# Moving weight preparation, a decay chain of one operation less, and two sets of folded DFT inputs in a fused attention, gated and mixing kernel

## The chip, the cores and the metric

The kernel runs on one core of a Trainium2 chip. The metric is the device time of one execution, in microseconds. Lower is better. The engines are TensorE (PE, with its weight loads shown as PEld), VectorE (DVE), ScalarE (ACT), GpSimd (POOL) and SyncE (SP), which here issues nearly all DMAs.

## The reference

Three layers run one after the other on 4 batches of 576 tokens. The first is causal attention with 8 heads of 64 dimensions, where a score also gets a decay: the difference of running sums of log f.

```python
cum = np.cumsum(np.log(np.clip(f, 0.0001, 1.0)), axis=-1)
scores = scale * np.matmul(q, k.transpose(0, 1, 3, 2)) + cum[:, :, :, None] - cum[:, :, None, :]
attn_out = softmax(where(causal, -1e9, scores)) @ v
# gated layer, d_ff = 1024, conv = 3 taps over the tokens
h = np.maximum(x @ w_in, 0.0)
y = (h * sigmoid(conv(h, conv_w))) @ w_out
# mixing layer
u = y + np.real(fft(fft(y, axis=1), axis=2))
out = u + np.maximum(layernorm(u) @ w_ch1, 0.0) @ w_ch2
```

The weights are double precision in memory, and the kernel turns them into single precision on the chip ("decode").

## The kernel before

**Stages.** Attention runs over 16 pairs of heads: `score` (L688) does the score matmuls and the exponentials, `trans` (L750) transposes the probabilities and `pv` (L788) multiplies them by v. The decay enters the scores as a second matmul against `cum`, a tile made once at the start (L607 to L613): clip, logarithm, running sum, a product with -8, a rounded copy on ACT, and for two strips of 32 rows the remainder that the rounding left. After each four pairs (one batch) `bc_chunks` (L815) adds 24 chunks to a queue, which the loop feeds in between the pairs: 8 chunks `b_chunk` (x @ w_in, convolution, gate) and 16 halves of chunks `c_chunk` (the product with w_out). The result goes to memory as `z_d`. Then `dft` (L955) makes u for each batch: it loads `zz` tiles, folds them into `zo` and splits each into a rounded and a remainder part in `zh` (L963 to L972), multiplies `zh` by the DFT's matrices, evacuates to `ab`, multiplies again (`pq`), and writes u to `u_d`. The last part is the channel layer over chunks of 512 tokens (`prep_u`, `ch1`, `ch2`), with the fourth batch's DFT worked in.

**Weights.** `load_w_in` (L626) and `load_w_out` (L632) each handle one of 8 units. A unit is one DMA of 512 KB, then `decode` (one ACT and four DVE operations on 128x512), then for w_in a rounded copy on ACT and a remainder on POOL. For w_out there are, besides, a sum and a difference of mirrored columns (POOL and DVE) and a DMA that stores the unit to `wo_d`, from which `c_chunk` loads it again. `prep` (L894 to L897) hands two units of w_in to each of the first four half-steps of the pair loop, and two of w_out to each of half-steps 6 to 9. The preparation of the first 7 of 16 slices of w_ch1 and w_ch2 follows from half-step 10.

**What orders the work.** Nothing is issued in the order of the code. Every operation is recorded, and a planner (`Plan.order`, L448) lists them: for each engine it takes, of the operations that are ready by its own table of costs, the one whose latest start is earliest. An operation with a `hold` is not ready before that planned time (nanoseconds), and one with a `lead` counts as more urgent. The outcome is a fixed order for each engine's queue, and each queue runs strictly in that order. So a change at any place can move work elsewhere.

**Memory.** The tiles of `dft` lie in the pool `dp`, which takes the place of the attention's tiles when those are free. `zh` is one tile, and four `zz` tiles rotate. The pool `mr`, which holds the channel layer's weights and its inputs `ux`, `uc`, `uh` and `ul`, takes the place of the gated layer's pools `bc` and `ga`.

Of the kernel before, what the change touches and what calls it, by code (L numbers as in the profile page):

```python
# [7 lines left out]
F32 = mybir.dt.float32  # L8
F32R = mybir.dt.float32r
I32 = mybir.dt.int32  # L10
U32 = mybir.dt.uint32
AF = mybir.ActivationFunctionType
ALU = mybir.AluOpType
# [9 lines left out]
CUTS = (0, 8, 16)  # L23
NMR, G3 = 7, (2, 2)
ULE, W2E = 'V', 'V'
NCV, NZZ, NZO, NX = 2, 4, 2, 5
NUO, NWARM = 1, 10
LASTW = 256
EV = (2, 4)
NTV = 4  # L30
NPT = 1
DRAIN = 200.0
NS, NU, NSPLIT = 4, 2, 4
NPB = 2
BK3 = (3,)
# [8 lines left out]
UW, ZW = DM + 2, 640  # L44
# [172 lines left out]
def cost_of(eng, fn, kw, subs=None):  # L217
    if subs:
        return DRAIN + sum(cost_of(eng, f, k) for f, k in subs) / 2
    o = kw["out"]  # L220
# [295 lines left out]
def build(tc, qk, v, f, w_in, conv, w_out, w_ch1, w_ch2, c_mask, c_ident, c_sgn, c_dd, c_ds, out):  # L516
    plan = Plan(tc)
    V, A, G, T, SP = (Engine(plan, n) for n in ("DVE", "ACT", "POOL", "PE", "SP"))

    def dma(out, in_):  # L520
        SP.dma_start(out=out, in_=in_)

    def hi(out_, in_):
        A.activation(out=out_, in_=in_, func=AF.Copy)

    def lo(eng, out_, in_, hi_):
        eng.tensor_tensor(out=out_, in0=in_, in1=hi_.bitcast(F32), op=ALU.subtract)
# [39 lines left out]
    dp = plan.pool("dft", after=[att])  # L567
# [9 lines left out]
    z_d = [dram.tile([4, 128, ZW], F32) for _ in range(B)]  # L577
# [9 lines left out]
    cum = att.tile([128, S], F32R)  # L587
# [12 lines left out]
    ft = att.tile([128, S], F32, tag="rb")  # L600
# [6 lines left out]
    V.tensor_scalar(out=ft, in0=ft, scalar1=1e-4, scalar2=1.0, op0=ALU.max, op1=ALU.min)  # L607
    A.activation(out=ft, in_=ft, func=AF.Ln)
    V.tensor_tensor_scan(out=ft, data0=one, data1=ft, initial=0.0, op0=ALU.mult, op1=ALU.add)
    V.tensor_scalar(out=ft, in0=ft, scalar1=-8.0, scalar2=None, op0=ALU.mult)  # L610
    A.activation(out=cum, in_=ft, func=AF.Copy)
    for i in (32, 96):
        lo(V, cum[i:i + 32], ft[i:i + 32], cum[i:i + 32])  # L613
    plan.lead = 0.0
    dma(out=mask, in_=c_mask)
    dma(out=ident, in_=c_ident)
# [5 lines left out]
    def load_conv():  # L622
        t = decode(wp, fetch(wp, conv, 3 * NFO), 3 * NFO)
        V.tensor_scalar(out=cw, in0=t, scalar1=2.0, scalar2=None, op0=ALU.mult)
# [37 lines left out]
    for par in range(2 * NPB):  # L662
        row = []
        for i in range(5):
            w = KW[i] + 64
            t = att.tile([128, w], F32)
# [222 lines left out]
    def bc_step():  # L889
        if queue:  # L890
            queue.pop(0)()

    load_conv()
    prep = {}  # L894
    for u in range(8):
        prep.setdefault(u // 2, []).append((load_w_in, u))
        prep.setdefault(6 + u // 2, []).append((load_w_out, u))  # L897
    clear_pads()
    for s in range(NP + 1):
        if 2 * s == SCST:  # L900
            plan.hold = 1e4 * SCST
            for i in range(2):
                G.dma_start(out=dd_d[:, i], in_=c_dd[:, i])
            for i in range(2):
                G.dma_start(out=ds_d[:, i], in_=c_ds[:, i])
            plan.hold = 0.0
        for x in (2 * s, 2 * s + 1):
            for fn, u in prep.get(x, []):
                fn(u)
            if 10 <= x < 10 + NST:  # L910
                plan.bias = 1e6
                for k in range(2):
                    dma(out=wch_d[2 * (x - 10) + k], in_=fetch_ch(k, x - 10))
                plan.bias = 0.0
        load(s + 1)
        if s < NP:
            load_v(s)
        for grps, tiles in (((4, 1), TX), ((3, 2), TY)):
            for grp in grps if s >= 1 else ():
                for n in (2 * s - 2, 2 * s - 1):  # L920
                    trans(n, grp)
                bc_step()
                bc_step()
            if s < NP:
                for part in (tiles[:1], tiles[1:]) if s < NSPLIT else (tiles,):
                    score(s, part)
        if s < NP:
            norm(s)
        if s >= 1:
            pv(s - 1)  # L930
            if s % (H // 2) == 0:
                queue.extend(bc_chunks(s // (H // 2) - 1))
# [7 lines left out]
    def load_consts():  # L940
        for i in range(2):
            dma(out=cdh[:, i], in_=dd_d[:, i])
        for i in range(2):
            dma(out=cst[:, i], in_=ds_d[:, i])
# [2 lines left out]
    TT = [(0, 128), (128, 128), (256, 64)]  # L947
    SK = (128, 128, 33)

    zh = dp.tile([128, 2, 4, 289], F32R)  # L950
    uos = [dp.tile([128, 257], F32) for _ in range(NUO)]
    for t in uos:
        V.memset(out=t[:, 0:257:256], value=0.0)

    def dft(b, bank):  # L955
        zz = []
        for c in range(4):
            t = dp.tile([128, ZW], F32, tag="zz", bufs=NZZ)
            dma(out=t, in_=Flat(z_d[b], 128 * ZW * c, [ZW, 128], [1, ZW]))
            zz.append(t)  # L960
        if b == 0:
            load_consts()
        for c in (2, 0, 1, 3):  # L963
            zo = dp.tile([128, 5, 64], F32, tag="zo", bufs=NZO)
            zF, zB = zz[c].over(0, [128, 5], [1, 64]), zz[c].over(64, [128, 5], [1, 64])
            if c == 2:
                V.scalar_tensor_tensor(out=zo, in0=zB, scalar=sgn, in1=zF, op0=ALU.mult, op1=ALU.add)
            else:
                G.tensor_tensor(out=zo, in0=zF, in1=zB, op=ALU.subtract if c == 3 else ALU.add)
            z1 = zo.over(0, [1, 289])  # L970
            hi(zh[:, 0, c], z1)
            lo(G, zh[:, 1, c], z1, zh[:, 0, c])  # L972
# [284 lines left out]
```

## Time and profile before

| | us |
|---|---|
| median of 3 runs | 906.49 |
| lowest and highest of them | 905.81, 908.7 |
| the profiled execution | 901.2 |
| its span, first to last instruction | 899.4 |
| PE busy in the span | 848.3 (94%) |
| DVE, ACT, POOL busy | 534.6, 375.4, 195.6 |

All rows come from the profiled execution. Times in them are microseconds from the start of the span. A busy PE says only that a matmul was under way, and "PEclk" is the share of TensorE's full clock that was granted. "DMA" is the mean busy share of the 16 DMA engines. A row of the busy times by stage gives the stretch, its length, then for each engine the busy time and the count of its instructions, then PEclk, the DMA share and GB/s. A row of a timeline gives the start, the duration, the engine, the line, the operation and the tiles it writes <- reads; the brackets at its end tell how long the engine had been idle before it and what ended that. A row of a group ends with the count, the busy time, the mean of one in nanoseconds, and the idle time before it.

### The profile page before, as it was taken

What the parts mean: (1) busy time and instruction counts of PE and PEld (TensorE: products, weight loads), DVE (VectorE), ACT (ScalarE), POOL (GpSimd) and SP (SyncE); (2) the same over time, 40 slices, a digit from 0 to 9 for tenths busy, and PEclk for the clock granted to TensorE, in tenths of its full rate; (3) what the DMA queues carried; (4) which work ended last, traced back from release to release, by engine and by line L of the source; (5) the groups of instructions that cost most, each with busy time, mean ns of one, the idle gap of its engine ahead of it and who ended that gap; (6) DMA issues with size and microseconds to landing.
All of it is one profiled execution on the core that took longest, in us unless ns stands there. A gap on an engine that the chain in (4) does not pass through costs nothing.

```text
span 899.4 us, 14182 instructions
## 1 busy us (share of the span) xinstructions
PE 848.3 (94%) x5148; PEld 710.7 (79%) x5148; DVE 534.6 (59%) x1413; ACT 375.4 (42%) x1002; POOL 195.6 (22%) x204
## 2 busy tenths in 40 slices
PE   7787989899999999999996899999999999999998
PEld 6455878779887888899985788888888888888897
DVE  6887998478963684368647788884535112411141
ACT  5775876368645675365434443332121111111111
POOL 1233252102310231059636621110000000000000
PEclk9698999999999999999998999999999999999999
DMA  6465446973376204496679465442313000200010
GB/s 214 146 191 177 174 147 219 384 236 125 122 224 205 92 17 126 141 285 176 201 205 226 136 173 184 151 154 58 107 24 95 1 0 1 94 1 0 32 63 24
DMA packets 75270, 119.87 MB, mean 133 GB/s; under 512 B 10392, under 2 KB 44984, under 8 KB 75200
## 3 DMA queue, kind: packets, MB, share of 16 engines
q1 hardware_dynamic: 74624, 116.01, 42.6%
q0 software_dynamic: 576, 2.95, 0.9%
q8 instruction: 40, 0.66, 0.3%
q14 instruction: 30, 0.25, 0.1%
HBM read 93.66 MB, written 27.70 MB: 135 GB/s over the span
## 4 chain that ended last, share of the span: by engine, by line
PE 49%; DMA 5%; DVE 4%; POOL 3%; issue 2%; ACT 1%; SPq 0%; DVEq 0%; POOLq 0%; ACTq 0%
PE psc_c__4978 L506 11%; PE psc_c__4977 L506 10%; PE psc_c__5070 L506 4%; PE psc_c__5069 L506 4%; PE psdft_x__4025 L506 4%; PE psdft_x__4024 L506 4%; PE psc_c__5072 L506 3%; PE psc_c__5071 L506 3%; PE psbc_bc__529 L506 2%; PE psbc_bc__528 L506 2%; DMA dram_t__380<-glu_t__145 1%; DMA dram_t__381<-dft_u__3909 1%; PE psatt_u__179 L498 1%; DMA wprep_dw__121<-dram_t__384 1%; POOL dft_u__3909 L506 1%
## 5 line engine op out<-in xcount | busy, mean ns | idle before, releaser
L506 DVE SCALAR_TENSOR_TENSOR mr_gl__4869<-psc_c__4977,mr_gh__4868 128x512 fp32r<-128x512 f32 (+1 forms) x40 | 25.4, 635 | 89.8 <-ACT mr_gh__4868 L506 89.7
L506 ACT ACTIVATE mr_gh__4868<-psc_c__4977 128x512 fp32r<-128x512 f32 (+1 forms) x40 | 22.2, 555 | 124.2 <-PE psc_c__4977 L506 121.7
L506 DVE SCALAR_TENSOR_TENSOR mr_gl__4873<-psc_c__4978,mr_gh__4872 128x512 fp32r<-128x512 f32 (+1 forms) x40 | 25.3, 633 | 81.2 <-ACT mr_gh__4872 L506 81.1
L506 ACT ACTIVATE mr_gh__4872<-psc_c__4978 128x512 fp32r<-128x512 f32 (+1 forms) x40 | 22.2, 554 | 119.6 <-PE psc_c__4978 L506 114.7
L506 DVE SCALAR_TENSOR_TENSOR glu_cv__162<-glu_t__143,bc_t__127,glu_cv__162 128x576 f32<-128x576 f32 x32 | 33.8, 1055 | 7.3 <-ACT glu_cv__162 L506 7.0
L506 DVE SCALAR_TENSOR_TENSOR glu_cv__163<-glu_t__144,bc_t__127,glu_cv__163 128x576 f32<-128x576 f32 x32 | 33.0, 1031 | 3.2 <-ACT glu_cv__163 L506 3.0
L506 DVE TENSOR_SCALAR wprep_dw__118<-wprep_dw__118 128x512 f32<-128x512 f32 (+1 forms) x25 | 13.3, 532 | 26.9 <-ACT wprep_dw__118 L506 26.8
L498 PE MATMUL psatt_s__175<-att_t__67,att_t__66 64*128 64x288 f32 (+2 forms) x48 | 27.1, 564 | 1.1 <-DVE att_t__67 L506 1.1
L498 PE MATMUL psatt_s__176<-att_t__67,att_t__66 64*128 64x288 f32 (+2 forms) x48 | 27.1, 565 | 0.3 <-DVE att_t__67 L506 0.3
L506 ACT ACTIVATE wprep_dw__118<-wprep_dr__117 128x512 f32<-128x512 f32 (+1 forms) x21 | 13.7, 650 | 31.9 <-DMA wprep_dr__117<-in_moe_w_ch_dram 17.5
L506 ACT ACTIVATE wprep_dw__121<-wprep_dr__120 128x512 f32<-128x512 f32 x24 | 16.1, 670 | 22.2 <-DMA wprep_dr__120<-in_moe_w_ch_dram 13.2
L498 PE MATMUL psatt_u__179<-att_pt__101,att_tv__92 128*64 128x448 f32 (+3 forms) x80 | 23.1, 439 | 1.1 <-ACT att_pt__102 L506 1.1
L498 PE MATMUL psatt_u__179<-att_pt__102,att_tv__93 128*64 128x448 f32 (+3 forms) x80 | 23.1, 439 | 0.0
L498 PE MATMUL psatt_s__177<-att_t__67,att_t__66 64*128 64x288 f32 (+2 forms) x48 | 22.0, 465 | 0.0
L498 PE MATMUL psatt_s__178<-att_t__67,att_t__66 64*128 64x288 f32 (+2 forms) x48 | 21.9, 462 | 0.0
L498 PE MATMUL psatt_s__175<-att_qk__70 64*128 64x288 f32 (+2 forms) x48 | 19.7, 497 | 1.0 <-DVE att_nb__95 L506 1.0
L506 POOL TENSOR_TENSOR dft_u__3909<-dft_ue__3905,dft_t__3893 128x257 f32<-128x257 f32 (+3 forms) x20 | 17.0, 869 | 16.2 <-DMA dram_t__381<-dft_u__3909 13.4
L506 DVE COPY glu_t__145<-psbc_bc__529 128x256 f32<-128x256 f32 (+2 forms) x48 | 9.9, 258 | 16.9 <-PE psbc_bc__529 L506 16.9
L498 PE MATMUL psatt_u__174<-att_pt__101,att_tv__99 128*64 128x448 f32 (+4 forms) x72 | 19.3, 413 | 0.5 <-ACT att_pt__102 L506 0.5
L498 PE MATMUL psatt_s__176<-att_qk__70 64*128 64x288 f32 (+2 forms) x48 | 19.6, 495 | 0.0
L498 PE MATMUL psatt_u__174<-att_pt__102,att_tv__100 128*64 128x448 f32 (+4 forms) x72 | 19.3, 413 | 0.0
L498 PE MATMUL psatt_s__175<-att_qk__91 64*128 64x288 f32 (+2 forms) x48 | 18.6, 473 | 0.2 <-DVE att_nb__104 L506 0.2
(1456 smaller groups left out, 3166.1 us busy)
## 6 DMA issues: line engine op xcount, KB each, us to landing
bc_wo__138<-dram_t__376 SPq DMA_DIRECT2D x16, 512.0 KB
wprep_dr__120<-in_moe_w_ch_dram SPq DMA_DIRECT2D x16, 512.0 KB
wprep_dr__117<-in_moe_w_ch_dram SPq DMA_DIRECT2D x16, 512.0 KB
bc_wo__139<-dram_t__376 SPq DMA_DIRECT2D x16, 512.0 KB
att_qk__70<-in_qk_dram SPq DMA_DIRECT2D x8, 608.0 KB
att_qk__91<-in_qk_dram SPq DMA_DIRECT2D x8, 608.0 KB
att_rb__68<-dram_t__375 SPq DMA_DIRECT2D x32, 144.0 KB
wprep_dr__120<-in_moe_w_out_dram SPq DMA_DIRECT2D x8, 512.0 KB
```

The costliest lines, as they stand in the source:

```text
L498: getattr(eng[op.eng], f)(**{k: v.real() if isinstance(v, View) else v for k, v in kw.items()})
L506: getattr(eng[op.eng], op.fn)(**kw)
```

## The change

- **w_in by halves of its columns.** The four units with the first 512 columns come first, with no hold. The four with the last 512 columns are held until the planner's 30 us, and the load of the convolution's weights until its 20 us.
- **w_out later.** Its 8 units keep their half-steps, and are held until the planner's 60 us.
- **The decay.** The product with -8 is dropped as an operation of its own: the ACT copy gets a scale of -8, and the two remainders are made by an operation that multiplies by -8 and subtracts.
- **The DFT.** `zh` has two tiles in turn. Three `zz` tiles rotate in place of four, each is loaded directly ahead of its fold, in the order 2, 0, 1, 3, and the matrices' load is recorded behind the first of them.
- `H_CH` is 0.0, so nothing is held there.

```diff
--- before.py
+++ after.py
@@ -23,13 +23,14 @@
 CUTS = (0, 8, 16)
 NMR, G3 = 7, (2, 2)
 ULE, W2E = 'V', 'V'
-NCV, NZZ, NZO, NX = 2, 4, 2, 5
+NCV, NZZ, NZO, NX = 2, 3, 2, 5
 NUO, NWARM = 1, 10
 LASTW = 256
 EV = (2, 4)
 NTV = 4
 NPT = 1
 DRAIN = 200.0
+XW, H_IN, H_OUT, H_CH = 6, 3e4, 6e4, 0.0
 NS, NU, NSPLIT = 4, 2, 4
 NPB = 2
 BK3 = (3,)
@@ -607,10 +608,10 @@
     V.tensor_scalar(out=ft, in0=ft, scalar1=1e-4, scalar2=1.0, op0=ALU.max, op1=ALU.min)
     A.activation(out=ft, in_=ft, func=AF.Ln)
     V.tensor_tensor_scan(out=ft, data0=one, data1=ft, initial=0.0, op0=ALU.mult, op1=ALU.add)
-    V.tensor_scalar(out=ft, in0=ft, scalar1=-8.0, scalar2=None, op0=ALU.mult)
-    A.activation(out=cum, in_=ft, func=AF.Copy)
+    A.activation(out=cum, in_=ft, func=AF.Copy, scale=-8.0)
     for i in (32, 96):
-        lo(V, cum[i:i + 32], ft[i:i + 32], cum[i:i + 32])
+        V.scalar_tensor_tensor(out=cum[i:i + 32], in0=ft[i:i + 32], scalar=-8.0, in1=cum[i:i + 32].bitcast(F32),
+                               op0=ALU.mult, op1=ALU.subtract)
     plan.lead = 0.0
     dma(out=mask, in_=c_mask)
     dma(out=ident, in_=c_ident)
@@ -890,11 +891,11 @@
         if queue:
             queue.pop(0)()
 
-    load_conv()
     prep = {}
-    for u in range(8):
-        prep.setdefault(u // 2, []).append((load_w_in, u))
-        prep.setdefault(6 + u // 2, []).append((load_w_out, u))
+    for k in range(8):
+        prep.setdefault(k // 2, []).append((load_w_in, 2 * k if k < 4 else 2 * k - 7, H_IN if k > 3 else 0.0))
+        prep.setdefault(XW + k // 2, []).append((load_w_out, k, H_OUT))
+    prep[0].append((lambda u: load_conv(), 0, 2e4))
     clear_pads()
     for s in range(NP + 1):
         if 2 * s == SCST:
@@ -905,13 +906,14 @@
                 G.dma_start(out=ds_d[:, i], in_=c_ds[:, i])
             plan.hold = 0.0
         for x in (2 * s, 2 * s + 1):
-            for fn, u in prep.get(x, []):
+            for fn, u, plan.hold in prep.get(x, []):
                 fn(u)
+            plan.hold = 0.0
             if 10 <= x < 10 + NST:
-                plan.bias = 1e6
+                plan.bias, plan.hold = 1e6, H_CH
                 for k in range(2):
                     dma(out=wch_d[2 * (x - 10) + k], in_=fetch_ch(k, x - 10))
-                plan.bias = 0.0
+                plan.bias = plan.hold = 0.0
         load(s + 1)
         if s < NP:
             load_v(s)
@@ -947,22 +949,19 @@
     TT = [(0, 128), (128, 128), (256, 64)]
     SK = (128, 128, 33)
 
-    zh = dp.tile([128, 2, 4, 289], F32R)
     uos = [dp.tile([128, 257], F32) for _ in range(NUO)]
     for t in uos:
         V.memset(out=t[:, 0:257:256], value=0.0)
 
     def dft(b, bank):
-        zz = []
-        for c in range(4):
-            t = dp.tile([128, ZW], F32, tag="zz", bufs=NZZ)
-            dma(out=t, in_=Flat(z_d[b], 128 * ZW * c, [ZW, 128], [1, ZW]))
-            zz.append(t)
-        if b == 0:
-            load_consts()
+        zh = dp.tile([128, 2, 4, 289], F32R, tag="zh", bufs=2)
         for c in (2, 0, 1, 3):
+            zz = dp.tile([128, ZW], F32, tag="zz", bufs=NZZ)
+            dma(out=zz, in_=Flat(z_d[b], 128 * ZW * c, [ZW, 128], [1, ZW]))
+            if b == 0 and c == 2:
+                load_consts()
             zo = dp.tile([128, 5, 64], F32, tag="zo", bufs=NZO)
-            zF, zB = zz[c].over(0, [128, 5], [1, 64]), zz[c].over(64, [128, 5], [1, 64])
+            zF, zB = zz.over(0, [128, 5], [1, 64]), zz.over(64, [128, 5], [1, 64])
             if c == 2:
                 V.scalar_tensor_tensor(out=zo, in0=zB, scalar=sgn, in1=zF, op0=ALU.mult, op1=ALU.add)
             else:
```

## Rows read from the trace of the kernel before

**Rows 1.** Busy time of each engine by stage, granted clock (PEclk), DMA share.

```profile
0.00:60.00 60.00, 47.87 (x275) 32.85 (x277) 45.76 (x160) 39.90 (x119) 14.48 (x34) 0.86 0.55 178
60.00:140.00 80.00, 69.33 (x521) 55.94 (x519) 70.67 (x174) 57.89 (x169) 33.16 (x25) 0.96 0.53 175
140.00:280.00 140.00, 129.31 (x1006) 111.39 (x1005) 101.67 (x284) 83.92 (x273) 25.79 (x19) 1.00 0.67 223
280.00:460.00 180.00, 177.15 (x1367) 160.09 (x1366) 111.23 (x249) 97.47 (x270) 73.13 (x71) 1.00 0.53 152
460.00:520.00 60.00, 49.05 (x270) 41.17 (x270) 43.12 (x82) 25.04 (x46) 34.41 (x42) 0.94 0.74 183
520.00:899.40 379.40, 375.62 (x1718) 309.30 (x1716) 162.12 (x468) 71.17 (x126) 14.60 (x13) 1.00 0.23 68
```

**Rows 2.** Timeline, 5 to 12 us: start us, us, operation [idle before, releaser].

```profile
6.86 0.46 DVE L506 TENSOR_SCALAR att_rb__68<-att_rb__68 128x576 f32<-128x576 f32 x1
...
8.47 0.67 ACT L506 ACTIVATE wprep_dw__121<-wprep_dr__120 128x512 f32<-128x512 f32 x1 [1.73 <-DMA wprep_dr__120<-in_moe_w_in_dram]
...
9.15 0.67 ACT L506 ACTIVATE att_t__67<-att_rb__68 128x576 fp32r<-128x576 f32 x1
...
9.73 0.21 ACT L506 ACTIVATE att_t__66<-att_t__65 128x32 fp32r<-128x32 f32 x1
...
10.09 1.53 DVE L506 TENSOR_TENSOR att_t__67<-att_rb__68,att_t__67 32x576 fp32r<-32x576 f32 x2
...
10.98 0.37 PE L498 MATMUL psatt_s__175<-att_t__67,att_t__66 64*128 64x288 f32 x1 [1.11 <-DVE att_t__67 L506]
```

**Rows 3.** Groups by shape, 0 to 140 us: preparing w_in and w_out.

```profile
L506 ACT ACTIVATE wprep_dw__121<-wprep_dr__120 128x512 f32<-128x512 f32 x9 | 6.0, 670 | 3.6 <-DMA wprep_dr__120<-in_moe_w_in_dram 3.4 <-DMA wprep_dr__120<-in_moe_w_out_dram 0.3
...
L506 DVE TENSOR_SCALAR wprep_dw__121<-wprep_dw__121 128x512 f32<-128x512 f32 x9 | 4.4, 491 | 4.6 <-ACT wprep_dw__121 L506 4.6
...
L506 DVE TENSOR_SCALAR wprep_de__122<-wprep_dw__121 128x512 int32<-128x512 int32 x9 | 5.0, 555 | 0.0
...
L506 DVE SCALAR_TENSOR_TENSOR wprep_dw__121<-wprep_dr__120,wprep_de__122 128x512 int32<-128x512 int32 x8 | 5.5, 685 | 0.0
...
L506 DVE SCALAR_TENSOR_TENSOR wprep_dw__121<-wprep_dr__120,wprep_dw__121 128x512 int32<-128x512 int32 x8 | 5.5, 687 | 0.0
...
L506 DVE TENSOR_TENSOR wprep_de__119<-wprep_dw__121 128x255 f32<-128x255 f32 x4 | 1.6, 411 | 0.0
...
L506 POOL TENSOR_TENSOR wprep_dr__117<-wprep_de__119,wprep_dr__117 128x512 fp32r<-128x512 f32 x8 | 11.6, 1445 | 19.7 <-ACT wprep_dr__117 L506 16.1 <-issue 3.6
```

**Rows 4.** Timeline of SP's DMA issues, 43 to 128 us.

```profile
43.04 0.33 SPq L506 DMA_DIRECT2D wprep_dr__120<-in_moe_w_out_dram  x1
...
51.15 0.33 SPq L506 DMA_DIRECT2D wprep_dr__120<-in_moe_w_out_dram  x1
...
114.75 0.57 SPq L506 DMA_DIRECT2D wprep_dr__120<-in_moe_w_out_dram  x1
...
127.74 0.39 SPq L506 DMA_DIRECT2D wprep_dr__120<-in_moe_w_ch_dram  x1
```

**Rows 5.** Timeline of PE, 130 to 140 us: the first matmul with w_out.

```profile
137.10 0.54 PE L506 MATMUL psbc_bc__528<-glu_t__146,bc_wo__138 128*128 128x288 f32 x2
```

**Rows 6.** Timelines of DVE and POOL, 100 to 140 us.

```profile
111.45 2.62 POOL L506 TENSOR_TENSOR wprep_dr__117<-wprep_de__119,wprep_dr__117 128x512 fp32r<-128x512 f32 x1 [2.46 <-issue]
...
112.86 1.83 DVE L506 SCALAR_TENSOR_TENSOR glu_cv__162<-glu_t__143,bc_t__127,glu_cv__162 128x576 f32<-128x576 f32 x1
...
118.08 0.81 DVE L506 SCALAR_TENSOR_TENSOR glu_cv__163<-glu_t__144,bc_t__127,glu_cv__163 128x576 f32<-128x576 f32 x1
```

**Rows 7.** Timelines of PE, SP and DVE, 470 to 482 us.

```profile
480.31 0.42 PE L506 MATMUL psdft_x__4024<-dft_t__3890,dft_t__3892 128*33 128x256 f32 x1 [4.76 <-ACT dft_t__3892 L506]
...
472.79 0.85 SPq L506 DMA_DIRECT2D mr_ux__4855<-dram_t__381  x2
...
481.66 0.71 DVE L506 STREAM_TRANSPOSE mr_uc__4856<-mr_ux__4855 128x512 f32<-128x512 f32 x1 [3.26 <-DMA mr_ux__4855<-dram_t__381]
```

## The prediction

> **What bounds the kernel now.** I read the busy times by stage first. From 520 us on PE is busy for 375.62 of 379.40 us at full clock, and from 280 to 460 us for 177.15 of 180 [rows 1]. There PE's own work sets the time, and the change takes no matmul away. So nothing can be won there, and a second won ahead of it arrives at the end unchanged. The idle time of PE lies in four places: 12.1 us before 60 us, 10.7 from 60 to 140, 10.7 from 140 to 280, 10.9 from 460 to 520 [rows 1]. Before 60 us the granted clock is 0.86 in the mean, so PE was for a part of the time at the lower of its two levels (1.2 in place of 2.4 GHz), which costs up to (1 - 0.86) x 60 = 8.4 us there.
>
> Next, the engine that PE leans on. DVE is busy for 45.76 of the first 60 us and for 70.67 of the next 80, where only 9.3 us are left [rows 1]. The preparation of w_in and w_out runs there among the scores' work. Then the timelines: the start, where the decay chain stands [rows 2], and 470 to 482 us, where PE stands for want of the last batch's fold and of the channel layer's input [rows 7].
>
> **The change part by part.**
>
> *The decay chain.* The product with -8 took 0.46 us of DVE at 6.86 us, so the rounded copy could have begun at 7.32. It began at 9.15, behind the decode of a w_in unit that had kept ACT idle for 1.73 us waiting for its DMA [rows 2]. ACT's queue runs in its written order, so with the same order the 0.46 us is hidden by that wait and the gain is 0. If the planner now puts the copy ahead of the decode, it can start at 6.86, where the product starts now. It takes 0.67, the two remainders took 1.53 together, so they would end at 9.06 in place of 11.62. PE was free from 9.87 (10.98 less 1.11 idle), so the gain is then at most 11.62 - 9.87 = 1.75 us, and less if the copy from the mask at 9.73 has its data late [rows 2]. The new remainder does the same elements in one operation of the same two inputs. I price it like the old one, 1.53/2 each. Its neighbour in form, a scalar_tensor_tensor of 576 columns, took 0.81 [rows 6], which would add 0.1 for the two. I take 0.5 us, nearer the lower end, because the row shows the order in which the copy stands behind.
>
> *w_in.* A unit costs ACT 0.67 for its first step and DVE 0.49 + 0.56 + 0.69 + 0.69 = 2.43 [rows 3]. Four units, 9.7 us of DVE, may not begin before 30 us, and the convolution's weights not before 20. But they are due at the fifth chunk of the first batch, so they stay ahead of about 110 us, and most of them inside the first 60 us. Unit by unit the earlier half has the same instructions and the same DMA of 512 KB. I cost this move at nothing by itself: DVE's 14.2 idle us before 60 [rows 1] hold it, and without that cover it costs up to 2 units, 4.9 us.
>
> *w_out.* A unit costs DVE 2.43 + 0.41 = 2.84, besides one small product, and POOL 1.45 for its remainder, besides the sum [rows 3]. Eight loads were issued from 43.04 to 114.75 us, two of them before 60, at 43.04 and 51.15 [rows 4]. These two leave the first 60 us: 5.7 us of DVE. What PE gains from that lies between 0 (DVE had idle time anyway) and 5.7 x 45.76/60 = 4.3, the share of the time in which DVE is busy. I take half, 2.2. The work comes back after 60 us, where DVE has 9.3 us left and PE 10.7. The cost there is 0 at best. At worst it is 5.7 x 70.67/80 = 5.0. Cover exists: the first w_ch load is issued at 127.74 [rows 4], and w_ch is not used before the channel layer, so two of its units (4.9 us of DVE) can step aside. I take 0.7. Net 1.5, between -5.0 and 4.3. The loads go through SP with their stores. The last load at 114.75 came 22 us ahead of the first matmul with w_out at 137.10 [rows 4, 5]. That is the margin. Once it is used up, the `wo_d` stores and the loads of `wo` behind them make PE wait.
>
> *The DFT.* Two `zh` tiles let a batch be folded while the batch before is still being multiplied. Up to 460 us that is worth nothing, as PE is covered by chunks of the gated layer [rows 1]. After the last chunk, PE stood 4.76 us at 480.31 for the fourth batch's last fold, and the first transpose for the channel layer waited until 481.66 for `ux`, loaded at 472.79 [rows 7]. The second tile makes neither of these earlier: the last `zz` load hangs on the last chunk's store, and `ux` lands in memory that the gated layer had held. But the third batch's multiplications need no longer be done before the fourth's folds, so the planner may leave them for this gap. That is worth 0 to 4.8, or up to 10.9 if the whole stage fills [rows 1]. Against it stands the third `zz` tile: the load for block 3 now waits for the fold of block 2, and SP's queue with the `zt` and `ab3` transfers stands behind it. It is a DVE operation already due, so I price that wait at 0 to 1 us, hidden by the chunks up to 460 us. I take a gain of 1.5, since the planner's order for this gap cannot be read from any row.
>
> The sum is 0.5 + 1.5 + 1.5 = 3.5 us, so the profiled execution would go from 901.2 to 897.7. The median of the runs is 906.49, 5.3 us above that execution, and I take the same 3.5 from it: **903.0 us**.
>
> **The rivals.** A measurement of this kernel can tell about 0.3%, 2.7 us, from no change.
>
> *Nothing comes through.* The decay stays behind the w_in decode, DVE's work is only moved within the 140 us that must hold it, and the gap at 480 us is set by two DMAs that nobody moved. For it: DVE is busy for 116.4 of the first 140 us, and all of w_out must lie in them. Then 904 to 909, around 906.
>
> *The tail closes.* The planner fills the gap after the last chunk: 4.8 us at 480 and up to 5 of the rest of the stage, together with the start's 2. Against it: `ux` still comes at 481. That is 7 to 13 us, 893.5 to 899.5.
>
> *w_out falls on the gated layer (slower).* Between 100 and 140 us a POOL remainder of w_out started at 111.45 and took 2.62 where the mean is 1.45, and the convolution's DVE operation of 112.86 took 1.83 where its twin at 118.08 took 0.81 [rows 3, 6]. So the two stretched each other by about 1 us. If three more units of w_out fall there, DVE gets 3 x (2.84 + 1.0) = 11.5 us more, against about 1 us that was idle and 4.9 of w_ch that can leave: 5.6 us longer, less what the first 60 us gain (2.2), plus up to 2 where `wo` comes late. That gives 3 to 6 us more, 909.5 to 912.5. It decides when more than five of the eight units are decoded after 100 us. Before it was three.
>
> The Trainium skill, "SBUF — State Buffer", section "Who interferes with whom", has a rule that speaks for this rival: a DVE instruction with two SBUF inputs and a GpSimd instruction that reads SBUF exclude each other for a whole instruction. The pair at 111.45 and 112.86 agrees with it.
>
> **How the numbers follow.** The forecast, 2.7 to 6 us won, has 0.32, and the tail closing has 0.20; both are faster by over 0.3%, together 0.52. Nothing coming through has 0.28. The slower rival has 0.20, since the hold is on w_out itself and 22 us of margin is two of the units' mean spacing, (114.75 - 43.04)/7 = 10.2 us. The likeliest case alone spans 900.5 to 903.8. The range takes in the tail's closing but for its end, and two thirds of the slower rival: 893.5 to 911.5. About 0.05 lies below and 0.08 above.
>
> **What would show it.** Right: the copy to `cum` starts at about 7 us, no w_out load before about 60 us, PE's idle time before 60 us at about 10 us, and PE saturated from an earlier time than 520. Wrong: the copy again behind a decode that waits; DVE without idle time from 100 to 140 us and PE's idle time there well above 3 us, or waits of PE for `wo`; the stage after the last chunk as long as before. The prediction falls if the planner's new order moves something that no part here names, for instance the chunks against the pairs between 140 and 280 us, where 10.7 us of idle time are open to either side [rows 1].

## The result, and the profile after

| | before | after |
|---|---|---|
| median of 6 runs each, us | 906.47 | 899.36 |
| lowest and highest | 904.73, 911.54 | 896.56, 902.01 |
| profiled execution, its span | 901.2, 899.4 | 902.01, 900.2 |
| PE busy in the span | 848.3 | 851.9 |

The ratio is 0.9907 with an interval of 0.9884 to 0.993: 7.1 us faster, where 3.5 was forecast. The two profiles do not show this as a difference of their spans, because that of before is faster than each of the six runs of before and that of after is the slowest of its six. So what follows compares stretches and not ends. Runs that lie more than 1.5% above the fastest of their kernel are left out of its median and ratio, which concerns three of the eleven runs of `dft_only` below, its profiled one among them.

The busy times by stage, after:

```profile
0.00:60.00 60.00, 51.03 (x351) 36.55 (x352) 50.68 (x180) 45.15 (x146) 13.77 (x33) 0.97 0.58 190
60.00:140.00 80.00, 69.52 (x535) 56.23 (x531) 69.42 (x177) 57.41 (x178) 29.41 (x24) 0.96 0.52 162
140.00:280.00 140.00, 131.36 (x966) 113.98 (x968) 102.74 (x269) 80.41 (x247) 28.68 (x22) 0.95 0.69 225
280.00:460.00 180.00, 174.01 (x1329) 158.74 (x1328) 110.64 (x239) 94.61 (x264) 74.25 (x72) 0.99 0.54 158
460.00:520.00 60.00, 49.53 (x261) 41.35 (x260) 43.54 (x83) 25.06 (x46) 28.57 (x39) 0.93 0.85 179
520.00:900.20 380.20, 376.42 (x1718) 310.16 (x1716) 162.25 (x467) 70.73 (x126) 16.64 (x15) 0.99 0.21 65
```

Against [rows 1] the first row is the one that differs most. PE did 351 instructions in the first 60 us in place of 275. Its idle time there fell from 12.1 to 9.0 us and its granted clock rose from 0.86 to 0.97. In the four rows below it, PE's idle time moves both ways: 10.7 to 10.5, 10.7 to 8.6, 2.8 to 6.0, 10.9 to 10.5.

Where in the first 60 us this happens is seen in a finer cut by stretches of 4 us, first before, then after:

```profile
20.00:24.00 4.00, 2.33 (x22) 1.72 (x21) 4.00 (x12) 3.12 (x13) 0.26 (x1) 1.00 0.34 124
24.00:28.00 4.00, 3.79 (x12) 2.12 (x13) 3.64 (x21) 3.67 (x10) 2.25 (x2) 0.57 0.69 228
28.00:32.00 4.00, 2.16 (x10) 1.05 (x6) 2.64 (x6) 2.60 (x10) 0.00 (x0) 0.50 0.20 34
32.00:36.00 4.00, 3.65 (x18) 2.85 (x19) 3.53 (x10) 2.79 (x10) 2.31 (x2) 0.50 0.96 304
```

```profile
20.00:24.00 4.00, 3.28 (x22) 1.84 (x19) 3.58 (x20) 4.00 (x16) 2.51 (x2) 1.00 0.52 176
24.00:28.00 4.00, 3.94 (x32) 2.91 (x33) 3.19 (x14) 4.00 (x18) 0.00 (x0) 1.00 0.38 103
28.00:32.00 4.00, 3.37 (x26) 1.89 (x26) 4.00 (x23) 4.00 (x18) 0.00 (x0) 1.00 0.32 129
32.00:36.00 4.00, 4.00 (x40) 2.65 (x36) 3.54 (x14) 3.87 (x13) 1.28 (x1) 1.00 0.67 224
```

Before, PE was busy for only 2.33 of the 4 us from 20 us on, and then the clock stood at 0.50, the lower level, for 8 us and more. From 32 to 36 us it was busy for 3.65 us and did 18 instructions, where after it was busy for 4.00 and did 40. So busy time by itself does not tell how far PE came.

What PE waited for is seen in the trace of before, first just ahead of the lower clock, then at 28 us:

```profile
23.04 0.62 ACT L506 ACTIVATE bc_t__126<-wprep_dw__121 128x512 fp32r<-128x512 f32 x1
23.56 0.22 ACT L506 ACTIVATE att_pt__101<-psatt_u__174 128x64 f32<-128x64 f32 x1
23.83 0.55 PE L506 MATMUL psatt_u__174<-const_t__61,att_t__73 128*128 128x128 f32 x3 [1.21 <-ACT att_pt__101 L506]
...
28.95 0.66 ACT L506 ACTIVATE wprep_dw__118<-wprep_dr__117 128x512 f32<-128x512 f32 x1 [1.25 <-DMA wprep_dr__117<-in_moe_w_in_dram]
29.51 0.25 ACT L506 ACTIVATE att_rt__98<-psatt_u__179 10x128 f32<-10x128 f32 x1
...
29.81 1.11 PE L506 MATMUL psatt_u__179<-const_t__61,att_t__80 128*128 128x128 f32 x4 [0.77 <-ACT att_rt__98 L506]
```

At 23.83 PE had waited 1.21 us for a copy on ACT that stood behind the rounding of a w_in unit. At 28.95 a decode of w_in, at the head of ACT's queue, had waited 1.25 us for its DMA. An attention operation stood behind it, and PE waited 0.77 us for that.

The effect on the other engines is seen on ACT. The row followed here, called the first pair's product below (the rounding of `xh` from `att_xr`, the first input of the gated layer), is this before, with the row ahead of it, then after:

```profile
43.04 0.63 ACT L506 ACTIVATE bc_t__126<-wprep_dw__121 128x512 fp32r<-128x512 f32 x1 [0.42 <-DVE wprep_dw__121 L506]
44.83 0.69 ACT L506 ACTIVATE bc_xh__128<-att_xr__108 128x576 fp32r<-128x576 f32 x1 [1.16 <-DVE att_xr__108 L506]
```

```profile
34.76 0.68 ACT L507 ACTIVATE wprep_dw__118<-wprep_dr__117 128x512 f32<-128x512 f32 x1
35.34 0.68 ACT L507 ACTIVATE bc_xh__128<-att_xr__108 128x576 fp32r<-128x576 f32 x1
```

It moved from 44.83 to 35.34 us. Seven decodes of w_in stood ahead of it on ACT before, four after. The other end of the chain, the first matmul of the channel layer, before and after:

```profile
483.33 1.22 PE L506 MATMUL psc_c__4977<-mr_uh__4857,mr_t__4866 128*128 128x512 f32 x2 [0.21 <-ACT mr_uh__4857 L506]
```

```profile
479.11 1.22 PE L507 MATMUL psc_c__4980<-mr_uh__4854,mr_t__4863 128*128 128x512 f32 x2 [0.85 <-ACT mr_uh__4854 L507]
```

So 4.2 us of the 9.5 are left where the last stage begins.

**A balance of PE.** In each trace the span is PE's idle time, plus what the lower clock costs, plus the work. A mean clock of 0.982 says that 0.018 of the full speed was missing, so the lower clock costs at most (1 - clock) times the span, and less where PE was idle anyway. Before: 51.1 idle, (1 - 0.982) x 899.4 = 16.2, together 67.3, which leaves 832.1. After: 48.3 and (1 - 0.977) x 900.2 = 20.7, together 69.0, which leaves 831.2. The work is about the same, and the two executions lost about the same. The gain is one of the medians. Over the 22 runs of before beside the first four experiments the median granted clock was 0.977, over the six of after 0.983. By this estimate the clock is up to 0.006 x 900 = 5.4 us of the 7.1, and the rest is idle time. How the gain splits is not shown more closely than that. The Trainium skill, "TensorE: Matmul & The Clock Gate", section "HAM oscillation — how this bites in real kernels", reckons the cost as the time at the lower level x (1 - 1.2/2.4). At half speed that time is twice the missing share, 2 x (1 - 0.982) x 899.4 = 32.4 us before, so it comes to the same 16.2. The remainders of 832.1 and 831.2 agree with it, but are no strong test.

Up to 60 us this balance reads: before 12.1 + 0.14 x 60 = 20.5 us lost, after 9.0 + 0.03 x 60 = 10.8. The lead of 9.7 us is about the 9.5 by which the first product moved. A third of it is idle time, two thirds are clock.

### The profile page after: what moved, and what is told of

It is laid out like the page before. It is cut to its first block, busy times and chain, and to the rows that moved or that the text cites. A ratio compares the mean times of both kernels' runs of the same rounds, so it can differ in the third digit from the quotient of the medians.

```text
span 900.2 us, 14183 instructions
## 1 busy us (share of the span) xinstructions
PE 851.9 (95%) x5148; PEld 717.0 (80%) x5148; DVE 539.3 (60%) x1412; ACT 373.4 (41%) x1002; POOL 191.3 (21%) x204
## 4 chain that ended last, share of the span: by engine, by line
PE 47%; DMA 6%; POOL 3%; DVE 3%; issue 2%; SPq 1%; ACT 1%; DVEq 0%; POOLq 0%
PE psc_c__4981 L507 10%; PE psc_c__4980 L507 10%; PE psc_c__5082 L507 4%; PE psc_c__5083 L507 4%; PE psdft_x__4025 L507 4%; PE psdft_x__4024 L507 4%; PE psc_c__5085 L507 3%; PE psc_c__5084 L507 3%; DMA dram_t__340<-dft_u__3920 2%; SPq L507 1%; PE psbc_bc__547 L507 1%; PE psbc_bc__548 L507 1%; DMA dft_zz__3908<-dram_t__337 1%; DMA wprep_dw__121<-dram_t__347 1%; DVE glu_cv__163 L507 1%
## 5 line engine op out<-in xcount | busy, mean ns | idle before, releaser
L499 PE MATMUL psatt_s__175<-att_t__67,att_t__66 64*128 64x288 f32 (+2 forms) x48 | 25.8, 538 | 3.1 <-DVE wprep_dw__121 L507 3.1
L499 PE MATMUL psatt_s__176<-att_t__67,att_t__66 64*128 64x288 f32 (+2 forms) x48 | 25.8, 536 | 0.0
L499 PE MATMUL psatt_u__179<-att_pt__101,att_tv__92 128*64 128x448 f32 (+3 forms) x80 | 21.6, 417 | 0.6 <-ACT att_pt__102 L507 0.6
L499 PE MATMUL psatt_u__179<-att_pt__102,att_tv__93 128*64 128x448 f32 (+3 forms) x80 | 21.6, 417 | 0.0
L499 PE MATMUL psatt_s__178<-att_t__67,att_t__66 64*128 64x288 f32 (+2 forms) x48 | 21.4, 451 | 0.0
L499 PE MATMUL psatt_s__177<-att_t__67,att_t__66 64*128 64x288 f32 (+2 forms) x48 | 21.2, 449 | 0.0
L507 DVE SCALAR_TENSOR_TENSOR wprep_dw__121<-wprep_dr__120,wprep_dw__121 128x512 int32<-128x512 int32 x24 | 21.0, 876 | 0.2
L507 DVE TENSOR_SCALAR wprep_dw__118<-wprep_dw__118 128x512 f32<-128x512 f32 (+1 forms) x25 | 11.5, 460 | 13.4 <-ACT wprep_dw__118 L507 13.0
L507 POOL TENSOR_TENSOR dft_u__3920<-dft_ue__3916,dft_t__3904 128x257 f32<-128x257 f32 (+3 forms) x20 | 16.9, 864 | 9.7 <-DMA dram_t__340<-dft_u__3920 7.8
L507 POOL TENSOR_TENSOR dft_u__3917<-dft_ue__3916,dft_t__3904 128x257 f32<-128x257 f32 (+3 forms) x20 | 17.0, 870 | 8.5 <-DMA dram_t__340<-dft_u__3917 7.7
L499 PE MATMUL psatt_s__175<-att_qk__70 64*128 64x288 f32 (+2 forms) x48 | 18.6, 471 | 0.0
L499 PE MATMUL psatt_s__176<-att_qk__70 64*128 64x288 f32 (+2 forms) x48 | 18.5, 470 | 0.0
```

What stands on the lines that cost most here:

```text
L499: getattr(eng[op.eng], f)(**{k: v.real() if isinstance(v, View) else v for k, v in kw.items()})
L507: getattr(eng[op.eng], op.fn)(**kw)
```

## The experiments

The table puts all kernels side by side. "First product" is the row of `xh` above, "decodes" those of w_in ahead of it on ACT, "lost" is PE's balance, idle time plus the cost of the lower clock, over the three stages up to 280 us, and the last column is the first matmul of the channel layer. The four columns come from one profiled execution each, the medians from the runs named. Ratios are to runs of before taken beside them. A profiled execution need not be a typical one: that of before took 901.2 us, that of `late_out_early_in` 909.41, the second slowest of its twelve.

| kernel | median us | ratio, interval | first product | decodes | lost to 280 | channel layer |
|---|---|---|---|---|---|---|
| before | 906.5 | | 44.8 | 7 | 45.1 | 483.3 |
| changed | 899.4 | 0.9907, 0.9884 to 0.993 | 35.3 | 4 | 40.1 | 479.1 |
| changed_again | 900.2 | 0.9932, 0.9906 to 0.9957 | 35.3 | 4 | 36.3 | 479.4 |
| weights_only | 899.3 | 0.9921, 0.989 to 0.9951 | 39.2 | 4 | 32.2 | 476.2 |
| weights_redrawn | 899.2 | 0.9899, 0.9877 to 0.992 | 38.9 | 3 | 37.4 | 476.7 |
| w_in_only | 899.3 | 0.9903, 0.9877 to 0.993 | 40.5 | 6 | 33.6 | 474.7 |
| w_out_only | 899.7 | 0.9914, 0.9889 to 0.9939 | 35.3 | 4 | 39.1 | 477.0 |
| mask_first | 902.2 | 0.9958, 0.9934 to 0.9982 | 37.1 | 4 | 38.8 | 480.4 |
| w_in_later_still | 904.1 | 0.9969, 0.9946 to 0.9992 | 36.2 | 2 | 44.9 | 482.9 |
| late_out_early_in | 904.3 | 0.997, 0.9943 to 0.9997 | 44.1 | 7 | 47.9 | 487.4 |
| w_in_late | 904.4 | 0.9981, 0.9953 to 1.001 | 36.8 | 1 | 47.0 | 483.6 |
| before_redrawn | 905.8 | 0.9976, 0.9955 to 0.9998 | 41.6 | 7 | 37.5 | 475.5 |
| decay_only | 909.7 | 1.0041, 1.0017 to 1.0066 | 49.6 | 9 | 46.8 | 484.9 |
| dft_only | 911.7 | 1.0045, 1.0012 to 1.0077 | | 9 | | |

**One part at a time.** `decay_only` has the hunk of the diff at L607 to L613 alone, `dft_only` the two hunks of `NZZ` and `dft` alone, `weights_only` those of `load_conv`, `prep` and its loop alone. `changed_again` is the changed kernel beside them.

> The kernel before with the change of the decay alone. By the prediction's sum: 0 to 1.75 us less, 0.5 taken, and 0 if the rounded copy still stands on ACT behind the decode that waits for its DMA. By the theory that the holds on the weights carry the change: within 2 us of the kernel before. By the theory of the order (any edit makes the planner draw another order, and the time goes up or down by some us whatever the edit): anywhere between 6 us less and 6 us more, with pairs and chunks at other places from the first 100 us on.

> The kernel before with the weights' part alone: w_in by halves, the second half held to 30 us, the convolution's weights to 20, w_out to 60. By the prediction's sum: 1.5 us less. By the theory that the holds carry the change: 5 to 8 us less, and the first pairs' products finish about 10 us earlier than before (35 in place of 45 us for the first), as in the changed kernel. By the theory of the order: anywhere within 6 us.

> The kernel before with the DFT's part alone: two sets of folded inputs, three input tiles each loaded ahead of its fold. By the prediction's sum: 1.5 us less, out of the gap after the last chunk. By the theory that the holds carry the change: within 2 us of the kernel before. If the DFT carries it: 5 us or more less, with less idle time of PE between 460 and 520 us.

> The changed kernel once more beside the parts: about 7 us less than before (ratio near 0.991). If parts add up, the three kernels above sum to this; by the theory of the order they do not.

The weights alone give the whole gain, though the first product came at 39.2 us and not at the expected 35. The decay and the DFT alone are each slower by 0.4%, which only the theory of the order had allowed for, and put on top of the weights they change nothing that can be told (0.9921 without them, 0.9932 with them). So the parts don't add. The DFT's edit concerns work from about 380 us on, yet it too raises the decodes ahead of the first product from 7 to 9. The planner lists all operations anew, and the order of the first 60 us comes out otherwise. That these two kernels cost time by the new order and not by the operation edited is likely, but not shown: `decay_only` also began its scores 0.7 us later, and the one trace of `dft_only` is from an execution of 919.37 us, so its stages are not compared.

In `decay_only` the copy to `cum` was put ahead of the decode, as the forecast's upper end supposed. Its timeline:

```profile
6.82 0.67 ACT L506 ACTIVATE att_t__67<-att_rb__68 128x576 fp32r<-128x576 f32 x1
...
10.52 0.66 ACT L506 ACTIVATE wprep_dw__121<-wprep_dr__120 128x512 f32<-128x512 f32 x1 [3.04 <-DMA wprep_dr__120<-in_moe_w_in_dram]
11.41 0.23 ACT L506 ACTIVATE att_t__66<-att_t__65 128x32 fp32r<-128x32 f32 x1 [0.23 <-DMA att_t__65<-in_mask_dram]
11.69 0.39 PE L498 MATMUL psatt_s__175<-att_t__67,att_t__66 64*128 64x288 f32 x1 [2.59 <-ACT att_t__66 L506]
```

The copy ran at 6.82 us, and PE still began at 11.69 where it had begun at 10.98 [rows 2]: next late was the copy from the mask. It stood behind a decode that waited 3.04 us for its DMA, and then waited another 0.23 us for the mask's own load.

**How much a new order alone moves.** One entry of the planner's table of delays was raised by 2 ns, in the kernel before and in the one with the weights' part:

```diff
-LAG = {"PE": {"ACT": 197.0, ...
+LAG = {"PE": {"ACT": 199.0, ...
```

> The kernel before with one number of the planner's table changed by 2 ns (the delay from PE to ACT, 197 to 199). Nothing else differs, but nearly every queue comes out in another order. By the theory of the holds: within 2 us of the kernel before. By the theory of the order: as far off as the decay alone was (some 4 us) or further, to either side. What it shows is the spread that any edit of this kernel brings with it, against which the other parts have to be read.

> The weights' part alone, with the same 2 ns in the planner's table. By the theory of the holds: again 5 to 8 us less than before, since the work still leaves the first 60 us in any order. By the theory of the order: the gain of 7 us was one draw, and this one lies anywhere within 6 us of the kernel before.

The queues of ACT, DVE, POOL and SP all come out in another order. The time moves by 0.2% in either (0.9976 to before, and 0.9899 where the weights' part without it had 0.9921; the intervals of these two overlap). `decay_only` and `dft_only` are new orders too, at 1.004. So a new draw of the order can be worth some 2 to 4 us here, and the weights' gain of 0.8 to 1.0% stands above that. One redraw of each kernel is few.

**Which of the two weights.** `w_in_only` takes the halves of columns and the holds of 30 and 20 us, `w_out_only` only the hold of 60 us (their two main lines each):

```diff
+        prep.setdefault(k // 2, []).append((load_w_in, 2 * k if k < 4 else 2 * k - 7, 3e4 if k > 3 else 0.0))
+        prep.setdefault(6 + k // 2, []).append((load_w_out, k, 0.0))
...
+        prep.setdefault(k // 2, []).append((load_w_in, k, 0.0))
+        prep.setdefault(6 + k // 2, []).append((load_w_out, k, 6e4))
```

> The kernel before with w_in by halves (second half held to 30 us) and the convolution's weights held to 20 us, w_out as before. By the prediction's sum: nothing by itself. If w_in carries the gain, since it clears DVE and ACT in the first 30 us: 4 to 7 us less, and the first product about 5 us earlier than 45. If w_out carries it: within 2 us, beyond the spread of the order.

> The kernel before with the hold of w_out to 60 us alone. By the prediction's sum: 1.5 us less, between 4.3 less and 5.0 more. If w_out carries the gain: 4 to 7 us less, with PE's idle time before 60 us near 9 in place of 12 us. If w_in carries it: within 2 us.

Either alone gives it all: 0.9903 and 0.9914, more than the 4 to 7 us expected of the one that carries it. The hold on w_out also moves w_in: in `w_out_only` its loads were issued at 3.06, 13.26, 16.39, 27.11, 32.36, 38.17, 45.94 and 51.91 us, before at 3.05, 13.23, 13.67, 22.38, 23.96, 31.97, 34.50 and 46.21. All the preparation shares two sets of buffers in the order recorded, so the likely reason is that a w_out due later leaves the w_in ahead of it less urgent.

For the last four runs the theories were these. Theory one: what counts is how many decodes stand ahead of the first pair's product. Up to here the time rose with them: 3 to 6, then 7, then 9. Theory two: what counts is that w_out leaves the first 60 us, or that w_in comes by halves of its columns.

**Late w_out with early w_in.** `w_out_only` with w_in due 20 us earlier:

```diff
             for fn, u, plan.hold in prep.get(x, []):
+                plan.lead = 2e4 if fn is load_w_in else 0.0
                 fn(u)
```

> The kernel before with w_out alone held back to 60 us on the planner's clock, and w_in given an earlier due time, so that seven of its decodes stand ahead of the first pair's product again (before: 7, with w_out held alone: 4). Theory one, what counts is how many w_in decodes stand ahead of the first pair's product on ScalarE and VectorE: the gain vanishes, 905 us or more, and the first product of a pair starts at 41 us or later. Theory two, what counts is that w_out leaves the first 60 us: the time stays at 899 to 900 us as with w_out held alone.

Theory two fell: w_out left the first 60 us (first load at 64.81), yet the ratio was 0.997 in place of 0.9914. Theory one had asked for 905 us or more and got 904.32, so it missed by a little. Seven decodes were ahead, the first product came at 44.1, and in the profiled execution the clock was low again:

```profile
20.00:40.00 20.00, 17.19 (x90) 10.87 (x88) 17.81 (x62) 15.07 (x51) 5.70 (x4) 0.66 0.49 176
```

The changed kernel has x145 at 1.00 in the same 20 us. But this execution had a mean clock of 0.977. The median over the twelve runs is 0.987, above the 0.977 of before, and their time is still only 0.3% shorter. So in most of them it was not the clock that took the gain, and what did is not seen here.

**w_in late without the rest.** The kernel before with a hold on w_in alone:

```diff
+        prep.setdefault(u // 2, []).append((load_w_in, u, 4e4 if u >= 1 else 0.0))
+        prep.setdefault(6 + u // 2, []).append((load_w_out, u, 0.0))
```

> The kernel before with all units of w_in but the first held back to 40 us, whole rows, and w_out left where it was, so that one decode stands ahead of the first pair's product. Theory one (decodes ahead of the first product): 896 to 899.5 us, first product at 38 us or earlier. Theory two (w_out must leave the first 60 us, or the order by halves of columns is what pays): 904 to 908 us as before. If w_in then holds up the gated layer instead, later products of pairs start later than before from 60 us on, and the time is 906 us or more.

```profile
20.00:40.00 20.00, 19.23 (x161) 13.52 (x159) 15.63 (x69) 15.57 (x62) 2.68 (x2) 1.00 0.42 136
60.00:140.00 80.00, 68.48 (x490) 53.64 (x489) 70.46 (x181) 56.54 (x173) 34.92 (x25) 0.90 0.51 167
140.00:280.00 140.00, 131.48 (x994) 115.03 (x994) 103.09 (x280) 84.15 (x260) 31.20 (x24) 0.96 0.69 226
```

Here theory one fell as a rule for the time. One decode stood ahead, the first product came at 36.8 us, PE did 161 instructions in these 20 us, the most of the kernels tested, and the time is 904.44, with an interval that takes in no change at all. By the balance 13.3 us were lost up to 60 us, where before had lost 20.5. That lead went in the next two stages: PE was idle for 11.5 us at a clock of 0.90 from 60 to 140 us (19.5 us lost, before 13.9) and for 8.5 us at 0.96 from 140 to 280 (14.1, before 10.7). In the latter its longest waits were these:

```profile
PE psbc_bc__529 L506 <- DMA bc_wo__139<-dram_t__334: 5.6, 2, 3.0
PE psbc_bc__529 L506 <- DMA bc_wo__138<-dram_t__334: 1.3, 1, 1.3
```

The w_in units were loaded up to 71.89 us (before: 46.21), w_out's last at 142.91 (before: 114.75), and the gated layer's second product waited 6.9 us for `wo`. But before had waited 5.5 us for it there too, so `wo` explains little of the loss. A start that was won on loads put off was lost again within 280 us. That the loads themselves took it back, when they were due, is likely and not shown: what held PE from 60 to 140 us was not followed.

**Held further.** The changed kernel with three steps of hold on w_in:

```diff
-... (load_w_in, 2 * k if k < 4 else 2 * k - 7, H_IN if k > 3 else 0.0))
+... (load_w_in, 2 * k if k < 4 else 2 * k - 7, (0.0, H_IN, 5e4)[(k > 0) + (k > 3)]))
```

> The changed kernel with w_in's quarters held back further: the first at once, the next three to 30 us, the rest to 50 us on the planner's clock. If every decode ahead of the first pair's product still costs, 896 to 898.5 us with the first product before 35 us; if the gain is used up once the first product starts before about 40 us, 899 to 901 us, as the changed kernel; if the projections of the later pairs then wait for w_in, 902 us or more.

The time fits only the last of the three, "902 or more", and not for the reason given there, w_in. Its lead at 60 us was nearly as large as the changed kernel's (11.5 us lost, 10.8 there). From 140 to 280 us it lost 22.8 us where the changed kernel lost 15.6, most of the difference in one place, on the timeline:

```profile
177.22 0.66 ACT L507 ACTIVATE wprep_dw__121<-wprep_dr__120 128x512 f32<-128x512 f32 x1 [13.77 <-DMA wprep_dr__120<-in_moe_w_ch_dram]
177.91 0.43 DVE L507 TENSOR_SCALAR wprep_dw__121<-wprep_dw__121 128x512 f32<-128x512 f32 x1 [11.42 <-ACT wprep_dw__121 L507]
...
178.72 0.62 DVE L507 TENSOR_TENSOR att_xr__69<-psatt_u__174,att_rb__68 128x448 f32<-128x448 f32 x1
...
179.39 1.11 PE L507 MATMUL psatt_u__174<-const_t__61,att_t__75 128*128 128x128 f32 x4 [9.08 <-DVE att_xr__69 L507]
```

These rows show the mechanism of this loss. A decode of w_ch, which nothing needed before the channel layer 300 us later, stood at the head of ACT's queue and waited 13.77 us for its DMA, issued at 164.10. DVE's next step of the decode stood at the head of its queue and waited for ACT. Behind it stood `att_xr`, and PE waited 9.08 us for that.

**The mask first.** The changed kernel in its order, with two operations moved where the planner hands it out:

```diff
         seq = self.order()
...
+        for eng, moved, ahead in (
+                ("SP", lambda o: o.kw["in_"] is self.mask_in, lambda o: name(o, "out").startswith("wprep")),
+                ("ACT", lambda o: o.kw["out"] is self.sel_out, lambda o: name(o, "out").startswith("wprep"))):
+            m, n = (first(lambda o, f=f: o.eng == eng and f(o)) for f in (moved, ahead))
+            if m > n:
+                seq.insert(n, seq.pop(m))
```

> The changed kernel in the planner's order as it is, but with the load of the mask put ahead of w_in's loads on SP and ScalarE's copy of the selection matrix put ahead of the first decode. The decay's first product should move from 12.2 us to 9.9 us or so. If the chain of the decay still sets the start, the whole is 1 to 2 us shorter than the changed kernel (898 us); if the start is covered by then, as the equal times of first products at 35 and 40 us suggest, it is the same within 0.3%: 898 to 901 us.

```profile
7.32 0.23 ACT L515 ACTIVATE att_t__66<-att_t__65 128x32 fp32r<-128x32 f32 x1 [0.68 <-DMA att_t__65<-in_mask_dram]
...
10.48 0.66 ACT L515 ACTIVATE wprep_dw__118<-wprep_dr__117 128x512 f32<-128x512 f32 x1 [2.93 <-DMA wprep_dr__117<-in_moe_w_in_dram]
11.05 0.67 ACT L515 ACTIVATE att_t__67<-att_rb__68 128x576 fp32r<-128x576 f32 x1
...
12.55 0.60 PE L507 MATMUL psatt_s__175<-att_t__67,att_t__66 64*128 64x288 f32 x1 [3.72 <-DVE att_t__67 L515]
```

The mask's copy came at 7.32 in place of 11.92, and the decay's first product did not come at 9.9 but at 12.55. The w_in load, now issued after the mask, landed later, and the copy to `cum` stood behind its decode. Moving one operand ahead made the other the late one. The median of 902.24 us lies above both expected cases, 898 and 898 to 901. The interval of its ratio, 0.9958, overlaps that of `changed_again`, so no difference between the two is shown.

**What the runs settle.** No kernel here is shown to beat the changed one. A gain of 0.4 to 1.0% came where w_in's decodes were thinned out ahead of the first pairs and the lead was still there at 280 us. By the balance up to 280 us, the kernels without a lead (before, `decay_only`, `late_out_early_in`, `w_in_late`, `w_in_later_still`, 44.9 to 47.9 us lost) take 904 to 910 us. Those with one (32.2 to 40.1) take 899 to 902, but for `before_redrawn`, which had lost 37.5 in its profiled execution of 901.96 us and has a median of 905.8. This split was found after the runs and not forecast, and it rests on one execution of each kernel. Which order keeps its lead can't be told from the holds: that stays open.

## Why the prediction was right, and where it was not

**What bounds the kernel** held in part. From 280 us on nothing was won. But that a second won ahead of it arrives at the end unchanged did not hold in this pair of traces. After was 4.2 us ahead at the channel layer's start, and from that matmul to the last instruction before took 416.1 us and after 421.1. Most of that lies here, before, then after:

```profile
515.00:530.00 15.00, 15.00 (x73) 12.58 (x72) 12.87 (x25) 7.98 (x14) 6.87 (x9) 1.00 0.79 201
```

```profile
515.00:530.00 15.00, 11.09 (x45) 9.14 (x45) 9.98 (x22) 6.34 (x11) 6.47 (x10) 0.77 0.53 126
```

```profile
517.02 0.63 ACT L507 ACTIVATE mr_t__4878<-wprep_dw__118 128x512 fp32r<-128x512 f32 x1 [1.37 <-DMA wprep_dw__118<-dram_t__352]
517.68 0.69 DVE L507 TENSOR_TENSOR mr_t__4878<-wprep_dw__118,mr_t__4878 128x512 fp32r<-128x512 f32 x1 [1.57 <-ACT mr_t__4878 L507]
...
519.35 1.55 PE L507 MATMUL psdft_x__4025<-dft_ab__3911,dft_t__3903 128*64 128x258 f32 x6 [3.92 <-DVE dft_ue__3916 L507]
```

A weight's preparation waited for its DMA on ACT, DVE waited for ACT, and PE waited 3.92 us for a DVE operation behind it.

**The decay**, priced at 0.5 us, gave nothing. The timeline after, against [rows 2]:

```profile
8.49 0.67 ACT L507 ACTIVATE wprep_dw__118<-wprep_dr__117 128x512 f32<-128x512 f32 x1 [1.84 <-DMA wprep_dr__117<-in_moe_w_in_dram]
9.06 0.67 ACT L507 ACTIVATE att_t__67<-att_rb__68 128x576 fp32r<-128x576 f32 x1
9.77 1.53 DVE L507 SCALAR_TENSOR_TENSOR att_t__67<-att_rb__68,att_t__67 32x576 fp32r<-32x576 f32 x2
...
11.92 0.23 ACT L507 ACTIVATE att_t__66<-att_t__65 128x32 fp32r<-128x32 f32 x1 [0.19 <-DMA att_t__65<-in_mask_dram]
12.20 0.40 PE L499 MATMUL psatt_s__175<-att_t__67,att_t__66 64*128 64x288 f32 x1 [3.13 <-DVE wprep_dw__121 L507]
```

The copy stayed behind the waiting decode, as the text took for likeliest, and the new remainders took the 1.53 us at which they were priced. But the copy from the mask came at 11.92 in place of 9.73, behind a second decode and a last wait of 0.19 us for the mask's load, and PE began 1.2 us later than before. The text named that copy and priced it only as a smaller gain.

**w_in, "I cost this move at nothing by itself"**, is the step that failed most. Alone it gave 0.9903, the whole gain. The text weighed it by DVE's capacity: 14.2 idle us would hold the units wherever they lie. But DVE was busier in the first 60 us after the change (50.68 for 45.76), and PE did more. What counted, by the rows at 23.04 to 29.81 us of before, was the units' place in queues that run in order, ahead of or behind the operations for which PE waits.

**w_out, net 1.5**, had the right sign and was sized too small: alone 0.9914, or 7.8 us of 908.6. The two ends of its gain, 0 to 4.3, held only DVE's time. The clock was missing. The first part had read that its 0.86 costs "up to 8.4 us" of lower level, and no term of the sum gave any of it back; by the balance, 6.6 us came back up to 60 us. Nor is the cause that it named seen. The 5.7 us of DVE's work were read off two loads, but the second of these units was decoded only from here on:

```profile
58.81 0.65 ACT L506 ACTIVATE wprep_dw__118<-wprep_dr__120 128x512 f32<-128x512 f32 x1
```

So about 3.2 us of w_out's work on DVE lay before 60 us, and DVE was busier there in `w_out_only` too (50.07 us for 45.76). The right sign was partly luck: the hold on w_out thinned out w_in, which the text did not think of. What it said of the loads was right. SP's issues after, against [rows 4]:

```profile
57.01 0.33 SPq L507 DMA_DIRECT2D wprep_dr__120<-in_moe_w_out_dram  x1
...
131.52 0.88 SPq L507 DMA_DIRECT2D wprep_dr__120<-in_moe_w_out_dram  x1
...
144.58 0.39 SPq L507 DMA_DIRECT2D wprep_dr__120<-in_moe_w_ch_dram  x1
```

w_out's first load left at 57.01, and w_ch stepped aside from 127.74 to 144.58, as the text supposed. **The slower rival** did not decide: the decode of four units began after 100 us, where it needed more than five. PE's idle time from 60 to 140 us stayed (10.7 and 10.5). Its fear, waits for `wo`, was real in before, with 5.5 us between 140 and 280; in the changed kernel there were none.

**The DFT, 1.5 us**, gave nothing that can be told. From 460 to 520 us PE was idle for 10.5 us where it had been 10.9. The two gaps of [rows 7] look like this after:

```profile
475.48 0.31 PE L507 MATMUL psdft_x__4024<-dft_t__3902,dft_zh__3924 128*33 128x256 f32 x1 [2.81 <-ACT dft_zh__3924 L507]
```

The wait for the last fold is 2.81 in place of 4.76, and `ux` was loaded at 468.15 in place of 472.79, 4.6 us earlier, about as much as the stage itself came earlier. **The tail closes** is thereby out as well. The last sentence of the forecast, that a new order could move something that no part names, fits `decay_only` and `dft_only`, and the wait at 519.35.

The sum's 3.5 us had the right sign through w_out, and the range, 18 us wide, held the result. Its make-up did not hold: the 7.1 is the weights' share alone, and w_in, which gives it alone, had been priced at nothing; at 60 us two thirds of the lead were clock, which the sum had no term for.

## What to carry to other kernels

Background work in an in-order queue is not priced by the capacity of its engine. Ask which operation stands right behind it, whether it can wait at the queue's head for a DMA, and who waits for that operation: a decode that nothing needs can stop three engines. Where PE stands at its lower clock, count the speed that is missing, (1 - clock) times the stretch, as a term of its own, and follow a lead stage by stage to the end. Where a planner orders everything, time an edit against a redraw of the order that changes nothing before crediting the operation.

## What was not expected

- A change of 2 ns in one entry of the planner's table reordered the queues and moved the median by 0.2%. An edit of work after 380 us changed the first 60 us.
- Between executions of one kernel the granted clock went from 0.977 to 0.989 and the time from 902.01 to 896.56 us with it. By the balance the clock could account for up to 0.012 x 900 = 10.8 us, twice the spread of 5.5, so the balance overstates what the clock costs between executions.
- In `w_in_later_still` a weight load of w_ch issued at 164.10 us released its decode only at 177.22, 13 us later.
